# A RetNet layer with a mixture-of-depths MLP: GpSimd drained ahead of the last MLP, one-hot rows ahead of values, another order of the first choice, and a limit on loads kept for the first batch alone

## The chip, the core and the metric

The kernel runs on one core of a Trainium2 chip. The core has a matrix engine (TensorE; PE in the profile, with its weight loads as PEld), a vector engine (VectorE, DVE), a scalar engine (ScalarE, ACT), GpSimd (POOL) and a queue that only issues transfers (SyncE, SP). The metric is the device time of one execution in microseconds, lower is better; a kernel is given by the median of its runs. A profile is one more execution, with a time of its own.

## What is computed

```python
# q, k, v: (8, 8, 576, 64); scale = 1/8
scores = scale * np.matmul(q, k.transpose(0, 1, 3, 2))
gamma = 1.0 - 2.0 ** (-5.0 - np.arange(H, dtype=np.float32))
Dmat = np.where(rel >= 0, gamma[:, None, None] ** rel[None, :, :], 0.0)
ret = np.matmul(scores * Dmat, v)            # (B, H, S, D) -> x: (B, S, H*D)

scores = np.einsum('bsd,d->bs', x, w_gate)   # x: (8, 576, 512)
for b in range(B):
    top_idx = np.argpartition(-scores[b], capacity)[:capacity]   # 128 of 576
    xe = x[b, top_idx]
    h = np.maximum(xe @ w1, 0.0)             # 512 -> 1024
    ye = h @ w2                              # 1024 -> 512
    g = 1.0 / (1.0 + np.exp(-scores[b, top_idx]))
    out[b, top_idx] = x[b, top_idx] + g[:, None] * ye
```

For each of eight batches: a linear attention with decay over 576 positions and eight heads, then a choice of the 128 positions with the highest gate score, an MLP on those alone, and its result added in place. All of it is in fp32.

## The kernel before

**Tiling.** A batch is cut into nine chunks of 64 positions (NC = 9), 72 chunks in all. One *step* s handles two chunks that follow each other, so there are 36 steps (NS) and a last, empty one. A batch has an odd number of chunks, so every second batch ends in the middle of a step. `ends[b]`, the step after the one that holds the last chunk of batch b, is 5, 9, 14, 18, 23, 27, 32, 36.

**A step.** `load(s)` brings q, k, v and k turned, four transfers of 256 KB through `bring` (L90) on SP's queue into one of eight `raw` buffers; the load of step s+7 is issued at the start of step s. `scaled(s)` (L137) multiplies v by decay factors on GpSimd (`vs`). `block(s)` (L195) puts the matmuls of step s on PE: the running state (`update`, `u_ps`), the scores (`sc_ps`), and, two by two in between, the products with v and state of the step before (`crosswise`, `y_ps`). ACT copies the state (`st`, L193). `masked(s)` (L218) masks the scores on DVE into `am`. `values(s-1)` (L224) scales `y_ps` into `xs` on DVE and sums each position's gate score (two `scr`, L235); `store(s-1)` (L239) writes `xs` out from GpSimd's queue.

**The choice of a batch.** `total` and `spread` lay the scores out as one row (PE, ACT). `compare` (L288, DVE) counts for every position how many are higher, in five pieces of up to 128 positions. `one_hot` (L303, DVE) turns ranks into a one-hot matrix, `rows` (L311, PE, then ACT) makes row numbers of it, `gather` (L322, GpSimd) fetches the chosen rows from the output. For the last step of a batch the compares are cut in two (`part`), joined by `joined`.

**The MLP.** `turn(b)` (L337) transposes the gathered rows on PE. `mlp(b)` (L370) appends eight *parts* to a queue: four `up` (L344), each 16 matmuls, and four `down` (L354), each 4. `some(n)` takes n parts from its front and issues them. `share` says how many parts each step takes. The last `down` of a batch is followed by DVE's `o` (L363) and an indirect scatter from GpSimd (L364). `gates(b)` (L328) makes the gate values.

**Order.** The scheduler is manual: each engine runs its instructions in the order in which the program issues them, and waits in that order. What belongs to a choice or an MLP is put in lists by step: `before` runs at the start of a step, `early` behind the step's block, values and store, `late` behind the parts of the MLP. The limit on loads is a dependency in `bring`: a transfer waits for the fourth one before it (`flying`). For a batch b from 1 to 6, with s = ends[b]: compares in `late` of steps s+1 (three) and s+2 (two), one-hot in `late` of s+2, row numbers and gather in `before` of s+3, the turn in `early` of s+4, parts from s+5. For batch 0: first compares behind step 4, rows and gather at the start of step 7, the turn in step 8. Behind step 36 come the second half of the choice of batch 7 between the parts of batch 6's MLP, then batch 7's MLP with nothing beside it.

At the end the program has, on every engine, instructions that it adds by itself (L547): drains and semaphores by which the engines meet, and SP's waits for the last transfers.

Of the kernel before, what the change touches and what calls it, by code (L numbers as in the profile page):

```python
# [9 lines left out]
F32 = mybir.dt.float32  # L10
# [3 lines left out]
OP = mybir.AluOpType  # L14
# [21 lines left out]
def kernel(  # L36
# [39 lines left out]
    def bank(name, tag="mm", bufs=3):  # L76
        return psum.tile([P, 512], F32, tag=tag, bufs=bufs, name=name)
# [2 lines left out]
    halves = [slice(0, C), slice(C, P)]  # L80
    where = lambda e, h: slice(W * e + D * h, W * e + D * h + D)
    batch = lambda g: divmod(g, NC)

    ctx.enter_context(tc.manual_schedule(engines=ENGINES))

# [1 line left out]

    flying = deque()

    def bring(out, in_):  # L90

        ins = nc.sync.dma_start(out=out, in_=in_).ins
        if len(flying) == 4:
            tc.add_manual_dep(
                ins, flying.popleft().name,
                mybir.DependencyInfo(mybir.DependencyClass.Sync, mybir.DependencyReason.DATA),
                reason="few transfers at a time")
        flying.append(ins)

    def load(s):  # L100
        x = loads.tile([P, 4, DM], F32, name="raw")
        for a in range(4):
            bring(x[:, a, :], qkvk[s, :, a * DM : (a + 1) * DM])
        raw[s] = x

    table = const.tile([P, col["end"]], F32, name="table")
# [27 lines left out]

    vs, am, sc_ps, y_ps, u_ps, st, xs, sc = {}, {}, {}, {}, {}, {}, {}, {}

    def scaled(s):  # L137
        c = batch(2 * s)[1]
        vs[s] = work.tile([P, DM], F32, name="vs")
        nc.gpsimd.tensor_tensor(  # L140
            out=blocks(vs[s]), in0=blocks(raw[s][:, 2, :]),
            in1=dec[:, 0, HH * c : HH * c + H].unsqueeze(2).to_broadcast([P, H, D]), op=OP.mult,
        )
# [22 lines left out]
                        raw[s][half, 0, where(e, h)],  # L166
                        start=True, stop=True, skip_group_check=True)

    def crosswise(s):
        y_ps[s] = bank("y_ps", "y", 2)  # L170
        for e in range(2):
            for h in range(HH):
                for i, half in enumerate(halves):
                    yield lambda e=e, h=h, i=i, half=half: nc.tensor.matmul(  # L174
                        y_ps[s][halves[1 - i], where(e, h)], am[s][half, where(e, h)],
                        vs[s][half, where(e, h)],
                        start=e == 0 and h == 0, stop=False, skip_group_check=True)
        for e in range(2):
            g = 2 * s + e
            if batch(g)[1] == 0:  # L180
                continue
            for h in range(HH):
                for i, half in enumerate(halves):
                    yield lambda g=g, e=e, h=h, i=i, half=half: nc.tensor.matmul(  # L184
                        y_ps[s][halves[1 - i], where(e, h)], raw[s][half, 0, where(e, h)],
                        st[g - 1][half, where(0, h)], start=False, stop=True,
                        skip_group_check=True)
# [7 lines left out]
    def block(s, cross=True):  # L195

        def diagonal():
            if s:
                yield from update(2 * s - 1)
            if s < NS:  # L200
                yield from scores(s)
                yield from update(2 * s)
        a = diagonal()
        b = crosswise(s - 1) if s and cross else iter(())
        n = 0
        while True:
            some = [f for f in (next(a, None), next(a, None), next(b, None), next(b, None)) if f]
            if not some:
                break
            for f in some:  # L210
                f()
            n += 1
            if n == HH and s:
                copied(2 * s - 1)
        if s < NS:
            copied(2 * s)

    def masked(s):  # L218
        am[s] = work.tile([P, DM], F32, name="am")
        nc.vector.tensor_tensor(  # L220
            out=blocks(am[s]), in0=blocks(sc_ps[s]),
            in1=causal.unsqueeze(1).to_broadcast([P, H, C]), op=OP.mult)

    def values(s):  # L224
        c = batch(2 * s)[1]
        xs[s] = work.tile([P, DM], F32, name="xs", bufs=4)
        nc.vector.tensor_tensor(  # L227
            out=blocks(xs[s]), in0=blocks(y_ps[s]),
            in1=dec[:, 1, HH * c : HH * c + H].unsqueeze(2).to_broadcast([P, H, D]), op=OP.mult)
        for e in range(2):  # L230
            b, c = batch(2 * s + e)
            if c == 0:
                sc[b] = work.tile([P, NC], F32, name="sc", bufs=2)
            scr = work.tile([P, W], F32, name="scr", bufs=1)
            nc.vector.scalar_tensor_tensor(scr, xs[s][:, W * e : W * e + W], 1.0, wgh,  # L235
                                           op0=OP.mult, op1=OP.mult,
                                           accum_out=sc[b][:, c : c + 1])

    def store(s):  # L239
        (b, c), (b2, _) = batch(2 * s), batch(2 * s + 1)  # L240
        for i, half in enumerate(halves):
            x = xs[s][half, :].rearrange("p (c d) -> p c d", c=2)
            if b == b2:
                nc.gpsimd.dma_start(  # L244
                    out=outs[b][C * c : C * c + 2 * C, W * i : W * i + W]
                    .rearrange("(c p) d -> p c d", c=2), in_=x)
            else:
                nc.gpsimd.dma_start(out=outs[b][C * c : C * c + C, W * i : W * i + W],
                                    in_=x[:, 0, :])
                nc.gpsimd.dma_start(out=outs[b2][:C, W * i : W * i + W], in_=x[:, 1, :])  # L250
# [127 lines left out]

    before, early, late = {}, {}, {}

    def plan(when, s, f, *a):
        when.setdefault(s, []).append((f, a))
# [3 lines left out]
            f(*a)  # L388

    columns = lambda k0, k1: [(k, 0, size(k)) for k in range(k0, k1)]  # L390
    ends = [(NC * b + NC - 1) // 2 + 1 for b in range(B)]
    last = B - 1
    odd = (NC - 2) // 2


    s = ends[0]
    plan(early, s - 1, total, 0, 0, NC - 1)
    plan(early, s - 1, spread, 0, columns(0, full))
    for k in range(full):
        plan(late, s - 1, compare, 0, k, 0, P * full)  # L400
    plan(early, s, total, 0, NC - 1, NC)
    plan(early, s, spread, 0, columns(full, NK))
    for k in range(full):
        plan(late, s, compare, 0, k, P * full, S, 1)
    plan(late, s, compare, 0, full)
    plan(late, s, joined, 0, full)
    plan(late, s, one_hot, 0)
    plan(before, s + 2, rows, 0)
    plan(before, s + 2, gather, 0)
    plan(early, s + 3, turn, 0)  # L410
    plan(early, s + 3, mlp, 0)
    plan(late, s + 3, gates, 0)
    start = [s + 3]
    for b in range(1, last):
        s = ends[b]
        plan(late, s, total, b)
        plan(early, s + 1, spread, b, columns(0, full), columns(full, NK))
        for k in range(NK):
            plan(late, s + 1 + (k > 2), compare, b, k)
        plan(late, s + 2, one_hot, b)  # L420
        plan(before, s + 3, rows, b)
        plan(before, s + 3, gather, b)
        plan(early, s + 4, turn, b)
        plan(late, s + 4, mlp, b)
        plan(late, s + 4, gates, b)
        start.append(s + 5)
    plan(late, NS - 1, total, last, 0, NC - 2)
    plan(before, NS, spread, last, columns(0, odd) + [(odd, 0, C)])
    for k in range(odd):
        plan(before, NS, compare, last, k, 0, C * (NC - 2))  # L430

    share = {}
    for s0, s1 in zip(start, start[1:]):
        n = s1 - s0
        for i in range(n):
            share[s0 + i] = 8 * (i + 1) // n - 8 * i // n

    AHEAD = 8
    bring(table, consts)
# [7 lines left out]
    for s in range(NS + 1):  # L447
        if s and s + AHEAD - 1 < NS:
            load(s + AHEAD - 1)
        if s == 2:  # L450
            for d in range(0, FB, 2):
                bring(w2_sb[:, d : d + 2, :],
                      w2[P * d : P * d + 2 * P].rearrange("(a p) d -> p a d", p=P))
        run(before, s)
        if s + 1 < NS:
            scaled(s + 1)
        block(s, s != ends[0])
        if s < NS:
            masked(s)
        if s and s != ends[0]:  # L460
            values(s - 1)
            store(s - 1)
        if s == ends[0] - 1:
            for f in crosswise(s):
                f()
        if s == 2:
            nc.vector.tensor_copy(out=place, in_=place_f)
        run(early, s)
        some(share.get(s, 0))
        if s == ends[0] - 1:  # L470
            values(s)
            store(s)
        run(late, s)
    some(1)
    total(last, NC - 2, NC)
# [11 lines left out]
    some(2)  # L487
    turn(last)
    some(len(parts))
    gates(last)  # L490
    mlp(last)
    some(len(parts))
# [58 lines left out]
```

## Time and profile before

| what | us |
|---|---|
| median of three runs (286.45, 288.38, 289.0) | 288.38 |
| the profiled execution | 286.14 |
| its span, first to last instruction | 284.4 |
| PE busy in it | 233.2 |
| DVE busy | 140.8 |
| GpSimd busy | 107.2 |
| ACT busy | 53.9 |

The difference between the profiled execution and its span, 1.7 us, lies outside the program's own instructions. PE's busy time counts matmuls that overlap; it is not work at full rate. The slices and windows below give busy time by stage, the granted clock is the share of TensorE's full clock, and the DMA share is the mean busy share of the core's 16 DMA engines. In a view of waits, a row names who waited, for whom, and the total, the number and the longest of the waits. An L with a number is a line of the kernel.

The groups of instructions whose durations the text uses:

```profile
L350 PE MATMUL h_ps<-xg,w_sb 128*128 128x128 f32 x512 | 64.0, 283 | 0.8 <-ACT xg L342 0.7
L140 POOL TENSOR_TENSOR vs<-raw,table 128x512 f32<-128x512 f32 x36 | 38.8, 1078 | 41.4 <-DMA raw<-in_qkvk 34.8
L227 DVE TENSOR_TENSOR xs<-y_ps,table 128x512 f32<-128x512 f32 x36 | 24.6, 684 | 8.1 <-PE y_ps L184 7.3
L364 POOL DMA_INDIRECT out<-o,idx x8 | 9.5, 1188 | 35.0 <-DVE o L363 29.3
```

In each row: line, engine, operation, what it writes and reads, shape, count; then busy us and mean ns of one; then the engine's idle time before it and who ended it. Matmuls of one group overlap, so a part of the MLP (16 of L350, or 4 of L358) takes 1.98 us of PE in the timeline, not 16 times 283 ns.

### The profile page before, as it was taken

The numbers are of one execution on the slowest core, as the hardware profiler recorded it, in microseconds if no ns is written. First come the engines' busy times: TensorE is split into PE (matmuls) and PEld (weight loads), VectorE is DVE, ScalarE is ACT, GpSimd is POOL, SyncE is SP. The second block draws the span as 40 slices with busy tenths as digits, with TensorE's granted clock in tenths as the row PEclk, the third lists the DMA queues.
The fourth block names the chain that finished last, engine by engine and source line by source line (L and its number), as shares of the span: only waits on it lengthen the run. The fifth ranks groups of instructions, "written<-read, shape, count | busy, mean of one in ns | idle before, by whom it ended". The sixth has DMA issues, their size and how long they took to land.

```text
span 284.4 us, 11522 instructions
## 1 busy us (share of the span) xinstructions
PE 233.2 (82%) x5184; PEld 186.5 (66%) x5184; DVE 140.8 (50%) x353; ACT 53.9 (19%) x158; POOL 107.2 (38%) x141
## 2 busy tenths in 40 slices
PE   1666773798789697999999979999999889999940
PEld 1656662697566696659866966688669856866710
DVE  0455793435746376456645773576366844331010
ACT  1111211132211131122211321132113212211100
POOL 4263722603663534343446516251647231111010
PEclk9998979579999998999999998999999999999996
DMA  6788999897888988988888855771313130201000
GB/s 218 237 275 294 293 318 345 273 362 252 279 289 281 309 261 265 300 289 277 256 307 269 293 200 180 268 223 42 76 44 96 38 85 13 76 11 63 2 37 0
DMA packets 27601, 56.83 MB, mean 200 GB/s; under 512 B 4000, under 2 KB 4128, under 8 KB 27552
## 3 DMA queue, kind: packets, MB, share of 16 engines
q1 hardware_dynamic: 22688, 42.46, 46.7%
q0 software_dynamic: 4864, 13.64, 14.1%
q8 instruction: 41, 0.67, 1.0%
q14 instruction: 8, 0.07, 0.1%
HBM read 44.54 MB, written 11.53 MB: 197 GB/s over the span
## 4 chain that ended last, share of the span: by engine, by line
PE 48%; DMA 23%; issue 14%; DVE 9%; POOL 2%; POOLq 1%; ACT 0%; DVEq 0%
DMA raw<-in_qkvk 18%; PE ye_ps L358 13%; PE h_ps L350 10%; PE u_ps L154 8%; PE sc_ps L164 7%; DMA w_sb<-in_w 4%; DVE scr L294 4%; PE row_ps L281 4%; PE y_ps L184 3%; PE y_ps L174 2%; DVE scr L235 2%; DVE xs L227 2%; DVE hot L307 1%; PE xg_ps L341 1%; DMA table<-in_consts 1%
## 5 line engine op out<-in xcount | busy, mean ns | idle before, releaser
L244 POOL DMA_DIRECT2D out<-xs x64 | 39.9, 625 | 67.6 <-DVE xs L227 67.2
L350 PE MATMUL h_ps<-xg,w_sb 128*128 128x128 f32 x512 | 64.0, 283 | 0.8 <-ACT xg L342 0.7
L220 DVE TENSOR_TENSOR am<-sc_ps,table 128x512 f32<-128x512 f32 x36 | 24.9, 691 | 76.5 <-PE sc_ps L164 56.8
L350 PEld LDWEIGHTS h_ps<-xg,w_sb 128*128 128x128 f32 x512 | 60.5, 196 | 3.3 <-ACT xg L342 1.1
L358 PE MATMUL ye_ps<-w_sb,hT 128*128 128x512 f32 x128 | 59.0, 601 | 0.5 <-issue 0.5
L164 PE MATMUL sc_ps<-raw 64*64 64x64 f32 x1152 | 45.9, 232 | 13.4 <-DMA raw<-in_qkvk 11.0
L154 PE MATMUL u_ps<-vs,raw 64*64 64x64 f32 x1024 | 46.7, 232 | 9.5 <-issue 4.5
L140 POOL TENSOR_TENSOR vs<-raw,table 128x512 f32<-128x512 f32 x36 | 38.8, 1078 | 41.4 <-DMA raw<-in_qkvk 34.8
L164 PEld LDWEIGHTS sc_ps<-raw 64*64 64x64 f32 x1152 | 41.5, 147 | 15.8 <-issue 15.8
L174 PE MATMUL y_ps<-vs,am 64*64 64x64 f32 x1152 | 47.0, 234 | 5.0 <-DVE am L220 3.2
L154 PEld LDWEIGHTS u_ps<-vs,raw 64*64 64x64 f32 x1024 | 38.6, 144 | 17.1 <-issue 9.8
L294 DVE SCALAR_TENSOR_TENSOR scr<-row,rs,ahead 128x576 f32<-128x576 f32 (+5 forms) x47 | 42.1, 895 | 12.2 <-ACT row L286 10.8
L174 PEld LDWEIGHTS y_ps<-vs,am 64*64 64x64 f32 x1152 | 40.7, 145 | 5.8 <-DVE am L220 3.1
L184 PE MATMUL y_ps<-st,raw 64*64 64x64 f32 x1024 | 41.5, 230 | 0.5 <-issue 0.5
L193 ACT COPY st<-u_ps 128x256 f32<-128x256 f32 x64 | 23.8, 372 | 91.9 <-PE u_ps L154 55.8
L358 PEld LDWEIGHTS ye_ps<-w_sb,hT 128*128 128x128 f32 x128 | 23.2, 192 | 23.7 <-issue 23.2
L184 PEld LDWEIGHTS y_ps<-st,raw 64*64 64x64 f32 x1024 | 37.6, 146 | 0.9 <-issue 0.8
L235 DVE SCALAR_TENSOR_TENSOR scr<-xs,table 128x256 f32<-128x256 f32 x72 | 32.4, 450 | 2.5
L227 DVE TENSOR_TENSOR xs<-y_ps,table 128x512 f32<-128x512 f32 x36 | 24.6, 684 | 8.1 <-PE y_ps L184 7.3
L363 DVE SCALAR_TENSOR_TENSOR o<-ye_ps,gate,xr 128x512 f32<-128x512 f32 x8 | 6.0, 751 | 34.1 <-PE ye_ps L358 21.4
L364 POOL DMA_INDIRECT out<-o,idx x8 | 9.5, 1188 | 35.0 <-DVE o L363 29.3
L352 ACT ACTIVATE hT<-h_ps 128x256 f32<-128x256 f32 x32 | 12.3, 384 | 49.6 <-PE h_ps L350 49.6
(34 smaller groups left out, 105.2 us busy)
## 6 DMA issues: line engine op xcount, KB each, us to landing
raw<-in_qkvk SPq DMA_DIRECT2D x144, 256.0 KB, 4.5
out<-xs POOLq DMA_DIRECT2D x64, 128.0 KB, 4.9
w_sb<-in_w SPq DMA_DIRECT2D x8, 512.0 KB, 5.5
out<-xs POOLq DMA_DIRECT2D x16, 64.0 KB, 5.1
wg<-in_w_gate SPq DMA_DIRECT2D x1, 256.0 KB
table<-in_consts SPq DMA_DIRECT2D x1, 234.5 KB
xr<-out,idx POOLq DMA_INDIRECT x8, 5.5
out<-o,idx POOLq DMA_INDIRECT x8
```

What stands on the lines that cost most here:

```text
L140: nc.gpsimd.tensor_tensor(out=blocks(vs[s]), in0=blocks(raw[s][:, 2, :]), in1=dec[:, 0, HH * c : HH * c + H].unsqueeze(2).to_broadcast([P, ...
L154: yield lambda h=h, half=half: nc.tensor.matmul(u_ps[b][half, where(0, h)], raw[s][half, 3, where(e, h)], vs[s][half, where(e, h)], start= ...
L164: yield lambda e=e, h=h, half=half: nc.tensor.matmul(sc_ps[s][half, where(e, h)], raw[s][half, 1, where(e, h)], raw[s][half, 0, where(e, h ...
L174: yield lambda e=e, h=h, i=i, half=half: nc.tensor.matmul(y_ps[s][halves[1 - i], where(e, h)], am[s][half, where(e, h)], vs[s][half, where ...
L184: yield lambda g=g, e=e, h=h, i=i, half=half: nc.tensor.matmul(y_ps[s][halves[1 - i], where(e, h)], raw[s][half, 0, where(e, h)], st[g - 1 ...
L220: nc.vector.tensor_tensor(out=blocks(am[s]), in0=blocks(sc_ps[s]), in1=causal.unsqueeze(1).to_broadcast([P, H, C]), op=OP.mult)
L227: nc.vector.tensor_tensor(out=blocks(xs[s]), in0=blocks(y_ps[s]), in1=dec[:, 1, HH * c : HH * c + H].unsqueeze(2).to_broadcast([P, H, D]), ...
L235: nc.vector.scalar_tensor_tensor(scr, xs[s][:, W * e : W * e + W], 1.0, wgh, op0=OP.mult, op1=OP.mult, accum_out=sc[b][:, c : c + 1])
L244: nc.gpsimd.dma_start(out=outs[b][C * c : C * c + 2 * C, W * i : W * i + W] .rearrange("(c p) d -> p c d", c=2), in_=x)
L294: nc.vector.scalar_tensor_tensor(scr[:n, : j1 - j0], row[b][:n, j0:j1], rs[b][:n, k : k + 1], ahead[:n, at + j0 : at + j1], op0=OP.subtrac ...
L350: nc.tensor.matmul(t[:, a, :], w1_sb[:, d, P * (f + a) : P * (f + a) + P], xg[b][:, d, :], start=d == 0, stop=d == KD - 1)
L358: nc.tensor.matmul(ye[b], hT[b][:, a, :], w2_sb[:, a, :], start=a == 0, stop=a == FB - 1)
```

## The change

Seven things, of which none changes what is computed:

1. `bring` gets an argument `few`. Only the loads of steps up to `ends[0]` = 5 wait for the fourth transfer before them; later loads and all weights don't.
2. `vs` of steps 5, 6 and 7 is made by ACT, in eight pieces a step, in place of GpSimd.
3. `crosswise` and `values` can do one chunk of a step alone, and steps 4 and 5 are written out as `first` and `second`: the chunk that ends batch 0 comes ahead of the one that begins batch 1, whose values stand behind batch 0's one-hot.
4. Batch 0's row numbers and gather go to step 6, its turn to step 7; its parts are taken from step 8 on, as before.
5. For batches 1 to 6 the last two compares and the one-hot go from behind a step's parts to ahead of its values (a new list, `mid`); row numbers and gather go from the start of the next step to the end of this one, behind the parts.
6. `mlp(b)` is queued in the step of its turn, and the shares are dealt earlier in each stretch, at most two a step, with the last part of a batch in the step in which the next batch's begin.
7. GpSimd drains between the scatter of batch 6 and the MLP of batch 7.

```diff
-    def bring(out, in_):
+    def bring(out, in_, few=False):
         ins = nc.sync.dma_start(out=out, in_=in_).ins
-        if len(flying) == 4:
+        while len(flying) > 3 + few:
+            flying.popleft()
+        if few and len(flying) == 4:
             tc.add_manual_dep(
...
-            bring(x[:, a, :], qkvk[s, :, a * DM : (a + 1) * DM])
+            bring(x[:, a, :], qkvk[s, :, a * DM : (a + 1) * DM], few=s <= ends[0])
...
+    by_act = lambda s: ends[0] <= s < ends[0] + 3
+
     def scaled(s):
...
+        if by_act(s):
+            for i in range(H):
+                nc.scalar.activation(
+                    out=vs[s][:, D * i : D * i + D], in_=raw[s][:, 2, D * i : D * i + D],
+                    func=AF.Copy, scale=dec[:, 0, HH * c + i : HH * c + i + 1])
+            return
...
-    def crosswise(s):
-        y_ps[s] = bank("y_ps", "y", 2)
-        for e in range(2):
+    def crosswise(s, es=(0, 1)):
+        if es[0] == 0:
+            y_ps[s] = bank("y_ps", "y", 2)
+        for e in es:
...
-    def values(s):
+    def values(s, es=(0, 1)):
...
+    def first():
+        s = ends[0] - 1
+        block(s)
+        masked(s)
+        go(crosswise(s, (0,)))
+        values(s - 1)
+        store(s - 1)
+        total(0, 0, NC - 1)
+        spread(0, columns(0, full))
+        values(s, (0,))
+        total(0, NC - 1, NC)
+        spread(0, columns(full, NK))
+        go(crosswise(s, (1,)))
+        for k in range(full):
+            compare(0, k, 0, P * full)
+
+    def second():
+        s = ends[0]
+        block(s, False)
+        masked(s)
+        for k in range(full):
+            compare(0, k, P * full, S, 1)
+        compare(0, full)
+        joined(0, full)
+        one_hot(0)
+        values(s - 1, (1,))
+        store(s - 1)
...
-    plan(before, s + 2, rows, 0)
-    plan(before, s + 2, gather, 0)
-    plan(early, s + 3, turn, 0)
-    plan(early, s + 3, mlp, 0)
-    plan(late, s + 3, gates, 0)
-    start = [s + 3]
+    s = ends[0] + 1
+    plan(mid, s, rows, 0)
+    plan(mid, s, gather, 0)
+    plan(early, s + 1, turn, 0)
+    plan(late, s + 1, mlp, 0)
+    plan(late, s + 1, gates, 0)
+    start = [s + 2]
     for b in range(1, last):
         s = ends[b]
...
-        for k in range(NK):
-            plan(late, s + 1 + (k > 2), compare, b, k)
-        plan(late, s + 2, one_hot, b)
-        plan(before, s + 3, rows, b)
-        plan(before, s + 3, gather, b)
+        for k in range(3):
+            plan(late, s + 1, compare, b, k)
+        for k in range(3, NK):
+            plan(mid, s + 2, compare, b, k)
+        plan(mid, s + 2, one_hot, b)
+        plan(late, s + 2, rows, b)
+        plan(late, s + 2, gather, b)
         plan(early, s + 4, turn, b)
-        plan(late, s + 4, mlp, b)
+        plan(early, s + 4, mlp, b)
         plan(late, s + 4, gates, b)
-        start.append(s + 5)
+        start.append(s + 4)
...
     share = {}
-    for s0, s1 in zip(start, start[1:]):
-        n = s1 - s0
-        for i in range(n):
-            share[s0 + i] = 8 * (i + 1) // n - 8 * i // n
+    for i, (s0, s1) in enumerate(zip(start, start[1:])):
+        n = 0
+        for s in range(s0, s1 + 1):
+            most = 1 if s == s1 or (i and s == s0) else 2
+            more = min(most, 8 - n - (s1 - s))
+            share[s] = share.get(s, 0) + more
+            n += more
...
-        if s + 1 < NS:
+        if s + 1 < NS and not by_act(s + 1):
             scaled(s + 1)
...
+        if s == ends[0] - 1:
+            first()
+        elif s == ends[0]:
+            second()
+        else:
+            block(s)
+            if s < NS:
+                masked(s)
+            run(mid, s)
+            if s:
+                values(s - 1)
+                store(s - 1)
...
+        if by_act(s + 1):
+            scaled(s + 1)
         run(early, s)
         some(share.get(s, 0))
         run(late, s)
...
     some(len(parts))
+    nc.gpsimd.drain()
     gates(last)
     mlp(last)
     some(len(parts))
```

More of the change, by code (lines that the diff above doesn't have):

```diff
@@ L82 @@
     batch = lambda g: divmod(g, NC)
+    ends = [(NC * b + NC - 1) // 2 + 1 for b in range(B)]
     ctx.enter_context(tc.manual_schedule(engines=ENGINES))
@@ L177, in crosswise @@
                         start=e == 0 and h == 0, stop=False, skip_group_check=True)
-        for e in range(2):
+        for e in es:
             g = 2 * s + e
@@ L222, in masked @@
             in1=causal.unsqueeze(1).to_broadcast([P, H, C]), op=OP.mult)
-    def values(s):
+    def values(s, es=(0, 1)):
         c = batch(2 * s)[1]
-        xs[s] = work.tile([P, DM], F32, name="xs", bufs=4)
+        if es[0] == 0:
+            xs[s] = work.tile([P, DM], F32, name="xs", bufs=4)
+        i0, i1 = HH * es[0], HH * es[-1] + HH
         nc.vector.tensor_tensor(
-            out=blocks(xs[s]), in0=blocks(y_ps[s]),
-            in1=dec[:, 1, HH * c : HH * c + H].unsqueeze(2).to_broadcast([P, H, D]), op=OP.mult)
-        for e in range(2):
+            out=blocks(xs[s])[:, i0:i1, :], in0=blocks(y_ps[s])[:, i0:i1, :],
+            in1=dec[:, 1, HH * c + i0 : HH * c + i1].unsqueeze(2).to_broadcast([P, i1 - i0, D]),
+            op=OP.mult)
+        for e in es:
             b, c = batch(2 * s + e)
@@ L377, in some @@
             f(*a)
-    before, early, late = {}, {}, {}
+    before, mid, early, late = {}, {}, {}, {}
     def plan(when, s, f, *a):
@@ L390, with go @@
     columns = lambda k0, k1: [(k, 0, size(k)) for k in range(k0, k1)]
-    ends = [(NC * b + NC - 1) // 2 + 1 for b in range(B)]
     last = B - 1
     odd = (NC - 2) // 2
[L396 to L407, printed above, removed]
-    plan(before, s + 2, rows, 0)
-    plan(before, s + 2, gather, 0)
-    plan(early, s + 3, turn, 0)
-    plan(early, s + 3, mlp, 0)
-    plan(late, s + 3, gates, 0)
-    start = [s + 3]
+    def go(fs):
+        for f in fs:
+            f()
+    def first():
[31 more added lines that the diff above has]
+    start = [s + 2]
     for b in range(1, last):
@@ L432 @@
     share = {}
-    for s0, s1 in zip(start, start[1:]):
-        n = s1 - s0
-        for i in range(n):
-            share[s0 + i] = 8 * (i + 1) // n - 8 * i // n
+    for i, (s0, s1) in enumerate(zip(start, start[1:])):
[5 more added lines that the diff above has]
+            n += more
+        assert n == 8
     AHEAD = 8
@@ L454 @@
         run(before, s)
-        if s + 1 < NS:
+        if s + 1 < NS and not by_act(s + 1):
             scaled(s + 1)
[L457 to L462, printed above, removed]
-        if s == ends[0] - 1:
-            for f in crosswise(s):
-                f()
+        if s == ends[0] - 1:
+            first()
[9 more added lines that the diff above has]
+                store(s - 1)
         if s == 2:
             nc.vector.tensor_copy(out=place, in_=place_f)
+        if by_act(s + 1):
+            scaled(s + 1)
         run(early, s)
         some(share.get(s, 0))
-        if s == ends[0] - 1:
-            values(s)
-            store(s)
         run(late, s)
```

## The prediction

> **What bounds the kernel now.** First the page's slices (7.1 us each): which engine is full in which stage.
>
> ```profile
> PE   1666773798789697999999979999999889999940
> PEclk9998979579999998999999998999999999999996
> DMA  6788999897888988988888855771313130201000
> ```
>
> From about the tenth slice on PE is full; before it, while the first loads come, it has holes. The last slice is empty: something behind the last matmul. So three stages, each read alone. The chain of waits for 40 to 67 us (start, length, what):
>
> ```profile
> 39.33 6.17 DMA w_sb<-in_w
> 45.52 4.82 DMA raw<-in_qkvk
> 50.36 4.10 DMA raw<-in_qkvk
> 54.47 5.77 DMA w_sb<-in_w
> 60.26 5.33 DMA raw<-in_qkvk
> 65.76 1.05 POOL vs L140
> ```
>
> Up to 65.8 us nothing but loads is on the path: step 8's load, step 9's, w2, step 10's. What the engines did there (busy times of PE, PEld, DVE, ACT, POOL; then the granted clock, the DMA share, GB/s):
>
> ```profile
> 40.00:50.00 10.00, 4.80 (x237) 4.10 (x234) 5.08 (x14) 1.65 (x5) 2.29 (x3) 1.00 0.96 348
> 50.00:65.00 15.00, 12.29 (x246) 11.04 (x235) 5.11 (x14) 4.16 (x10) 4.79 (x6) 0.66 0.91 311
> 65.00:111.00 46.00, 38.13 (x964) 31.26 (x965) 28.48 (x69) 9.21 (x27) 21.64 (x28) 1.00 0.86 280
> ```
>
> PE is half idle to 50, then works 12.3 of 15 us at a clock of 0.66. From 65 it is the bound: a load comes every 4.8 us, a step takes about 6.6 (block 10 starts at 65.1, block 35 at 229.5). What still stops it there, first from the waits of PE, then in the chain:
>
> ```profile
> PE idx_ps L315 <- DVE hot L307: 9.1, 7, 2.1
> ```
> ```profile
> 74.34 0.06 DVE am L220
> 74.95 0.69 DVE xs L227
> 75.67 0.44 DVE scr L235 x2
> 76.13 0.43 DVE scr L235 x2
> 76.56 0.75 DVE scr L294 x2
> 77.34 0.82 DVE scr L294 x2
> 78.16 0.61 DVE hot L307
> 78.82 0.37 PE idx_ps L315 x5
> ```
>
> PE's part of the MLP ends at 76.69 and PE waits 2.13 us for the one-hot, ahead of which DVE does the values of the step (xs and two scr: 1.6 us). The timeline has four such stops of 2.06 to 2.13 us (78.8, 110.9, 169.8, 228.7 us), 8.3 of the 9.1. Last, the instructions of the program's end (duration min/median/max, first and last start):
>
> ```profile
> L547 POOLq DRAIN  x3: 40/108/9130, 274.4 to 284.1; - x3
> L547 SPq DRAIN  x3: 7/7/7, 278.0 to 283.8; - x3
> ```
>
> GpSimd's first drain takes 9.13 us from 274.43, to 283.56. SP, which waits for the last scatter to land, is through at 278.0. So 5.5 us of the end are GpSimd's drain alone.
>
> **The change part by part.**
>
> *Drain ahead of the last MLP.* It adds a drain between the scatter of batch 6 (issued 260.60, 1.18 us) and that of batch 7 (274.66), which waits for DVE's o. Behind it on POOL is only that last scatter. Cover: 274.66 - 261.78 = 12.9 us. Scatters and gathers don't keep GpSimd: in the timeline a vs (L140) that follows an indirect one, and has its load, starts 1.02 to 1.26 us after it. So the 9.13 us are 1.2 us of scatter, the landing, and some 6 us of something else. The two drains behind it, with no transfer in between, took 108 and 40 ns. What one costs after a single transfer the trace does not show. If the time is per transfer since the start (96), the early drain takes it in the cover and the last one only waits for the landing: the end follows SP, -5.5. If it is owed behind any transfer, 0. A loss would need an early drain over 12.9 us; the one seen is 9.1. I take -5.5: its nearest rows are the short drains, which show that a drain as such is cheap.
>
> *Few loads for batch one only.* Before, each transfer on SP waits for the fourth before it. After, from step 6's loads on, that wait is gone; as built, SP's transfers take turns on eight semaphores, so each waits for the eighth before it: 2 MB in flight instead of 1 (SP's next wait, for a free raw buffer, is not near: it fills seven steps ahead). The four 512 KB pieces of w1 already had 2 MB in flight, in the window with share 0.96. The other windows are 0.89 (28 to 40 us) and 0.91 (50 to 65). Filled to 0.96: 12 x 0.07 + 15 x 0.05 = 1.6 us earlier for step 10's load (bounds 0, and 3.1 if filled to 1.00). It lands near 63.4 instead of 65.1.
>
> *First choice, and vs of steps 5 to 7 on ACT.* Half of the cross products and values of step 4 move behind the choice (DVE: half of 0.69, one scr of 0.44 with its 0.08: about 0.9 us), and the row numbers come in step 6, not 7. The gather, issued at 43.9, comes 3 to 4 us earlier and lands about 45; the turn (0.66 us of PE) moves from step 8 to the end of step 7. The 24 ACT pieces of 128x64, at the 217 ns of ACT's copy of that shape, take 1.74 us a step against 1.08 on POOL; if vs came last, that is 0.66 us each, so 0 to 2 us, or a small gain where DVE's compares no longer meet POOL's vs (one took 2.18 us at 32.5, its neighbours 0.75). I take 0: block 6 waits for DVE, blocks 7 and 8 for loads. By itself the choice is worth nothing for the end, loads being last.
>
> *Parts of the MLP.* Shares of batch 0 go from 1,1,2,1,1,2 (steps 8 to 13) to 2,2,1,1,1,1: two more parts of 1.98 us ahead of block 10. Is there room? From block 8 (49.3, some 0.9 earlier with the loads): two blocks of 2.1, four parts, 0.8 us of sums and gaps, 12.9 in all: block 10 could start at 61.3 and waits for its load until 63.4. With the half clock as before (10 us at half, 5 us of work lost) it starts at 66.3. Gain: 3.96 + 1.7 = 5.7, or 3.96 - 1.2 = 2.8. I take 4.5. From there PE is the bound and keeps it.
>
> *One-hot ahead of values.* In each choice of batches 1 to 6, compares and one-hot stand 1.6 us earlier on DVE; as built, the row numbers keep their place on PE, between a part and the next block, and the gather its place on POOL, ahead of the next vs. The four stops of 2.07 go to about 0.45: 6.4 us. The values behind come 2.5 us later; stores on POOL wait for them, and the gather behind the stores, so the gather gets little earlier. PE needs the freed y_ps two blocks later: no stop.
>
> *The clock.* The half clock of 3.4 us starts at 111.7 and at 169.7, right behind two of these stops (they end at 110.9 and 169.8); each loses 1.7 us of work. The Trainium skill, "TensorE: Matmul & The Clock Gate", Part 1, says the clock falls after an idle window of about 3.4 us; by that a 2 us stop should not do it and removing it would save nothing. The row shows the fall with 2 us of idle, so up to 3.4 us could come back; two other stops had none. I take 1.5.
>
> *The gathers.* Turn waits for the gather: in batch 1 it is issued at 79.66 and turned at 86.02, 6.4 us later, and it lands in
>
> ```profile
> DMA to landing us min/median/max: 4.7/5.5/6.1
> ```
>
> so slack is about 1 us, in other batches up to 3. If the spread of 1.4 us is what four loads in flight cost, eight make 7.5 at the most: a stop of about 1 us in some batches. The Trainium skill speaks against such a loss: "DMA: Bandwidth & Descriptors", Queues, rings and completion order, has each DMA engine take turns between its queues packet by packet, so a longer load queue would cost a gather nothing. By the rule 0, by the row up to -5 over four batches while loads run; I take a loss of 2.
>
> *Sum*: 5.5 + 4.5 + 6.4 + 1.5 - 2 = 15.9 us. The profiled execution took 286.14 (span 284.4); it becomes 270.2. The median shown is 288.38, 2.2 above it, so 272.5.
>
> **The rivals.** (1) The drain's time is owed behind the last transfer whatever was drained before. For: only one long drain is seen. Against: the short ones. 288.4 - 10.4 = 278. (2) The stops move: the one-hot is early, but late values, masks and gathers stop PE in its place, as DVE has 4.9 us in a one-part step of 4.5. Then 4.5 + 5.5 remain: 278.5. (3) Slower: gathers queue behind eight loads. Place: turn on PE, with a block behind it. 2 MB at 290 GB/s are 7 us, landing 12.5; less about 1.5 us of slack and the 5.5 known, 5.5 us each for batches 1 to 4, and 3 us in batch 0 (turn now stands ahead of block 8): 25 us against 17.9 of gains, 295.5. It decides from a landing of about 10.6 us. Against: landings never passed 6.1, with four loads in flight. (4) Neither drain nor stops give anything and the front alone is left, 4.5 - 2: 286, no change.
>
> **How the numbers follow.** Forecast 0.47, (1) 0.24, (2) 0.12, (3) 0.10, (4) 0.07. 1% (2.9 us) is about what a measurement of this kernel can tell. Faster 0.83, within 0.07, slower 0.10. The range, 263 to 284, takes in the drain at 0, the front at 2.8, and below the forecast the full 3.4 us of clock, no gather loss and a filled DMA; outside are (3), (4) and 0.05 below.
>
> **What would show it.** Right: the last drain under 3 us and the early one about 9, inside the last MLP; two parts more ahead of block 10; idx stops under 0.6 us. Wrong: a last drain of 6 us or more; gathers over 7 us with PE waiting at L341's like; block 10 not earlier in work done.

## The result, and the profile after

The changed kernel takes 274.1 us (median of four runs, 272.9 to 275.1), the kernel before 288.7 (four runs, 286.5 to 292.4). The ratio is 0.952, with a 95% interval of 0.944 to 0.960: faster, by 14.6 us between the medians where 15.9 were forecast. The profiled execution of the changed kernel took 274.87 us (span 273.2), so between the two profiled executions there are 11.3 us. Medians take in all runs and ratios only those within 1.5% of their kernel's fastest; two experiments below (the one-hot alone, and both edits with limited loads) have a slower run as their profile, so of the first only waits are read and of the second only the count of stops at the end.

The slices of the changed kernel (6.8 us each):

```profile
PE   1845886089977999969999999699999998999992
PEclk9998568569998999999999999979999999999998
DMA  6879999999996786586577766866042113211000
```

The front is not fuller than before: the eighth slice of PE is empty, and the fourth to the ninth have a granted clock under 0.9. The DMA engines are full from the fourth to the twelfth. The windows that were shown of before:

```profile
40.00:50.00 10.00, 5.37 (x213) 4.50 (x205) 6.54 (x20) 4.15 (x17) 2.82 (x5) 0.76 1.03 383
50.00:65.00 15.00, 9.37 (x256) 8.78 (x260) 3.12 (x9) 3.47 (x7) 6.57 (x9) 0.70 1.05 393
65.00:111.00 46.00, 42.61 (x1040) 33.79 (x1030) 27.91 (x66) 10.15 (x31) 19.23 (x25) 0.96 0.81 272
```

(A share over 1 means that counted times of packets overlap.) From 50 to 65 us loads run at 393 GB/s in place of 311, and PE is busy for less, 9.4 us in place of 12.3. From 65 on it is busier, 42.6 of 46 us in place of 38.1. The waits of PE say where the front went:

```profile
PE xg_ps L356 <- DMA xr<-out,idx: 12.6, 4, 7.5
PE sc_ps L175 <- DMA raw<-in_qkvk: 5.9, 1, 5.9
PE idx_ps L330 <- DVE hot L322: 3.2, 4, 1.4
```

Loads hold up PE once, at the very first block. Stops ahead of the row numbers are down from 9.1 us to 3.2. New is the first row: PE waits 12.6 us for gathered rows, 7.5 of it at once. The chain of waits has it as a transfer, ahead of the turn of batch 0:

```profile
48.73 6.85 DMA xr<-out,idx
55.63 1.11 PE xg_ps L356 x4
```

And the end, the early drain first, then those of the program's end:

```profile
L534 POOLq DRAIN  x1: 9263/9263/9263, 254.7 to 254.7; - x1
...
L592 POOLq DRAIN  x3: 46/108/3035, 268.8 to 272.9; - x3
L592 SPq DRAIN  x3: 7/7/7, 272.3 to 272.6; - x3
```

The early drain takes 9.3 us between the two scatters, the last one 3.0 and ends at 271.8, ahead of SP (272.3). DVE's last `o` starts at 268.0, 5.2 us before the end of the span; in the kernel before it started at 273.6, 10.7 us before the end.

### The profile page after: what moved, and what is told of

It is laid out like the page before. It is cut to its first block, busy times and chain, and to the rows that moved or that the text cites. A ratio compares the mean times of both kernels' runs of the same rounds, so it can differ in the third digit from the quotient of the medians.

```text
span 273.2 us, 11548 instructions
## 1 busy us (share of the span) xinstructions
PE 231.0 (85%) x5184; PEld 183.9 (67%) x5184; DVE 141.7 (52%) x354; ACT 58.7 (22%) x182; POOL 103.3 (38%) x138
## 4 chain that ended last, share of the span: by engine, by line
PE 60%; issue 14%; DMA 13%; DVE 8%; ACT 1%; POOLq 1%; POOL 1%; SPq 0%; DVEq 0%; ACTq 0%
PE h_ps L365 17%; PE ye_ps L373 11%; PE u_ps L165 9%; PE sc_ps L175 9%; DMA xr<-out,idx 7%; DVE scr L309 5%; DMA raw<-in_qkvk 5%; PE row_ps L296 5%; PE y_ps L196 4%; PE y_ps L186 3%; PE xg_ps L356 2%; DVE hot L322 1%; DVE am L232 1%; DMA out<-xs 1%; PE idx_ps L330 1%
## 5 line engine op out<-in xcount | busy, mean ns | idle before, releaser
L365 PEld LDWEIGHTS h_ps<-xg,w_sb 128*128 128x128 f32 x512 | 59.5, 192 | 5.5 <-issue 4.4
L373 PE MATMUL ye_ps<-w_sb,hT 128*128 128x512 f32 x128 | 63.0, 624 | 0.0
L365 PE MATMUL h_ps<-xg,w_sb 128*128 128x128 f32 x512 | 62.2, 278 | 0.5 <-issue 0.4
L175 PE MATMUL sc_ps<-raw 64*64 64x64 f32 x1152 | 44.9, 231 | 11.0 <-DMA raw<-in_qkvk 5.9
L186 PE MATMUL y_ps<-vs,am 64*64 64x64 f32 x1152 | 45.9, 232 | 3.0 <-issue 2.7
L165 PEld LDWEIGHTS u_ps<-vs,raw 64*64 64x64 f32 x1024 | 38.1, 144 | 11.7 <-issue 6.4
L196 PE MATMUL y_ps<-st,raw 64*64 64x64 f32 x1024 | 39.7, 227 | 2.0 <-issue 2.0
L151 POOL TENSOR_TENSOR vs<-raw,table 128x512 f32<-128x512 f32 x33 | 34.7, 1052 | 13.3 <-DMA raw<-in_qkvk 12.8
L196 PEld LDWEIGHTS y_ps<-st,raw 64*64 64x64 f32 x1024 | 36.0, 143 | 2.1 <-issue 2.1
L250 DVE SCALAR_TENSOR_TENSOR scr<-xs,table 128x256 f32<-128x256 f32 x72 | 34.0, 473 | 2.5
L241 DVE TENSOR_TENSOR xs<-y_ps,table 128x512 f32<-128x512 f32 (+1 forms) x37 | 24.7, 667 | 3.9 <-PE y_ps L196 3.6
L367 ACT ACTIVATE hT<-h_ps 128x256 f32<-128x256 f32 x32 | 12.3, 383 | 55.7 <-PE h_ps L365 55.7
```

The costliest lines, as they stand in the source:

```text
L151: nc.gpsimd.tensor_tensor(out=blocks(vs[s]), in0=blocks(raw[s][:, 2, :]), in1=dec[:, 0, HH * c : HH * c + H].unsqueeze(2).to_broadcast([P, ...
L165: yield lambda h=h, half=half: nc.tensor.matmul(u_ps[b][half, where(0, h)], raw[s][half, 3, where(e, h)], vs[s][half, where(e, h)], start= ...
L175: yield lambda e=e, h=h, half=half: nc.tensor.matmul(sc_ps[s][half, where(e, h)], raw[s][half, 1, where(e, h)], raw[s][half, 0, where(e, h ...
L186: yield lambda e=e, h=h, i=i, half=half: nc.tensor.matmul(y_ps[s][halves[1 - i], where(e, h)], am[s][half, where(e, h)], vs[s][half, where ...
L241: nc.vector.tensor_tensor(out=blocks(xs[s])[:, i0:i1, :], in0=blocks(y_ps[s])[:, i0:i1, :], in1=dec[:, 1, HH * c + i0 : HH * c + i1].unsqu ...
L365: nc.tensor.matmul(t[:, a, :], w1_sb[:, d, P * (f + a) : P * (f + a) + P], xg[b][:, d, :], start=d == 0, stop=d == KD - 1)
```

## The experiments

Each time stands beside runs of the kernel before on the same chip. On the three chips these had medians of 288.5, 290.4 and 291.0 us, so from chip to chip ratios are the better measure. "Block 10 starts" means its first scores, the first matmul that needs step 10's load.

**One part of the change at a time, on the kernel before.**

*The drain alone* (the diff is the one line `nc.gpsimd.drain()` ahead of `gates(last)`).

> The kernel before with the early drain alone. Theory (a drain pays for each transfer since the last one, the early one lies in the cover of the last MLP): last drain about 3 us, the early one about 9, time 5.5 us below before: 283 against 288.5. Rival (the 11 us of the whole change have little to do with it): under 3 us.

285.96 us, ratio 0.989 (0.982 to 0.996). The end of its profile:

```profile
L548 POOLq DRAIN  x3: 46/108/3043, 275.5 to 279.6; - x3
L548 SPq DRAIN  x3: 7/7/7, 279.1 to 279.4; - x3
```

The last drain is 3.0 us, as forecast, and GpSimd is ready ahead of SP. From the start of the last `o` to the end of the span there are 5.2 us, 5.5 less than before: the end gives what was forecast. The two profiled spans differ by 4.5 us, the medians by 4.4, the ratio says 1.2 to 5.1: 5.5 lies just outside. In this profile the loads of the front were later (step 10's landed at 68.0 us), which takes some of it back.

*The loads alone.*

```diff
-        if len(flying) == 4:
+        while len(flying) > 3 + few:
+            flying.popleft()
+        if few and len(flying) == 4:
...
-            bring(x[:, a, :], qkvk[s, :, a * DM : (a + 1) * DM])
+            bring(x[:, a, :], qkvk[s, :, a * DM : (a + 1) * DM], few=s <= 5)
```

> The kernel before with the limit on loads kept for steps 0 to 5 alone. Theory (loads bind the front of the kernel before, and with eight in flight they run at 360 to 390 GB/s there): step 10's load lands near 58 us in place of 64.7, block 10 starts about 5 us earlier, time 4 to 6 us below before. Rival (the wait moves to the turn of batch 0, whose gather now shares the engines with more loads, as in the changed kernel): block 10 starts at 64 or later, time within 2 us of before.

289.69 us, ratio 0.998 (0.989 to 1.007): nothing. The loads did speed up,

```profile
50.00:65.00 15.00, 13.65 (x328) 12.63 (x327) 5.54 (x15) 4.16 (x10) 5.60 (x7) 0.69 1.04 389
```

and step 10's landed at 57.3 us in place of 64.7; but block 10 started at 63.4, only 1.7 earlier, since PE was still at the parts and block 9 (granted clock 0.69). Up to 65 us PE also stood 9.1 us in stops that nothing in the profile explains, where before it stood 4.2 (the last section counts them). By 113 us, in batch 2's choice, the profile is 2.2 us behind that of before, after a stop of 4.2 us at 99.9 (told of at the end) and two more stretches of half clock. So where theory put the gain, PE itself was next, not a transfer; the rival named the turn of batch 0, and there PE did not wait.

*One-hot ahead of the values alone.*

```diff
-        for k in range(NK):
-            plan(late, s + 1 + (k > 2), compare, b, k)
-        plan(late, s + 2, one_hot, b)
-        plan(before, s + 3, rows, b)
-        plan(before, s + 3, gather, b)
+        for k in range(3):
+            plan(late, s + 1, compare, b, k)
+        for k in range(3, NK):
+            plan(mid, s + 2, compare, b, k)
+        plan(mid, s + 2, one_hot, b)
+        plan(late, s + 2, rows, b)
+        plan(late, s + 2, gather, b)
```

> The kernel before with, for batches 1 to 6, the last two compares and the one-hot ahead of the values and row numbers and gather behind the parts, nothing else. Theory: the four stops of 2.07 us of PE before the row numbers fall to 0.6 (6 us less), but the gathers go out 1.5 to 2 us later and PE stops at some turns: 3 to 5 us in all, so 1 to 3 us net, 286. Rival (no gather stop here): 6 us or more, 282.

286.31 us, ratio 0.985 (0.979 to 0.991), 4 us. Its waits of PE:

```profile
PE xg_ps L341 <- DMA xr<-out,idx: 5.3, 4, 2.9
...
PE idx_ps L315 <- DVE hot L307: 2.2, 4, 0.6
```

6.9 us of stops went ahead of the row numbers, and 4.9 came back at the turns (0.4 before). The first is as the theory has it, the second at the top of its 3 to 5. The net of 1 to 3 us was too low: the ratio says 2.5 to 6.2, so 2 lies outside.

*The shares of the parts alone.*

```diff
-        plan(late, s + 4, mlp, b)
+        plan(early, s + 4, mlp, b)
...
-        start.append(s + 5)
+        start.append(s + 4)
...
-        for i in range(n):
-            share[s0 + i] = 8 * (i + 1) // n - 8 * i // n
+        n = 0
+        for s in range(s0, s1 + 1):
+            most = 1 if s == s1 or (i and s == s0) else 2
+            more = min(most, 8 - n - (s1 - s))
+            share[s] = share.get(s, 0) + more
+            n += more
```

> The kernel before with the earlier shares of the MLP's parts alone (and a batch's parts queued in the step of its turn). Theory (two more parts ahead of block 10 fit into the time in which loads bind): four parts done when block 10 starts, block 10 not over 1 us later than at 65.1, 3 to 4 us below before. Rival (PE has no room there, as in the changed kernel): block 10 starts 3 to 4 us later and the time is within 1 us of before.

282.19 us, ratio 0.976 (0.967 to 0.985): the largest single part, 4 to 10 us. Block 10 starts at 65.8 us with four parts done, where before it started at 65.1 with two, and the window tells why there was room:

```profile
50.00:65.00 15.00, 14.33 (x243) 13.58 (x236) 5.10 (x14) 3.85 (x8) 3.95 (x6) 0.74 0.92 301
```

PE is busy 14.3 us of 15, before 12.3: the two parts fill the wait for step 10's load. They are 3.96 us, less the 0.7 by which block 10 is later: 3.2 of the 6.7 us between the two profiled spans. The other 3.5 come behind block 10, where the shares moved too; no run divides them.

**One part of the change taken back.** *All transfers limited to four, in the changed kernel* (`few` True for every transfer).

> The changed kernel with the limit of four kept for all transfers. Theory (in the changed kernel the front is bound by the turn of batch 0, not by loads): step 10's load lands near 65 us, ahead of block 10 (69.6 us in the changed kernel), time within 2 us of 274.1. Rival (the loads carry the gain of the front): block 10 later and 4 us or more above it, 278 to 280.

274.86 us, ratio 0.948 (0.936 to 0.959): the same as the changed kernel. Step 10's load landed at 66.1, ahead of block 10 at 68.6. PE's wait for gathered rows is 5.9 us longer and the time no worse; the unexplained stops of the last section are 3.8 us in this profile in place of 10.1.

```profile
PE xg_ps L356 <- DMA xr<-out,idx: 18.5, 6, 9.5
```

**What holds up the gathers.** GpSimd in the changed kernel's timeline, for batch 0:

```profile
30.98 0.53 POOL L263 DMA_DIRECT2D out<-xs  x1 [0.42 <-DVE xs L241]
42.19 0.53 POOL L265 DMA_DIRECT2D out<-xs  x1 [10.68 <-DVE xs L241]
42.71 0.52 POOL L263 DMA_DIRECT2D out<-xs  x1
43.22 0.52 POOL L265 DMA_DIRECT2D out<-xs  x1
48.73 1.03 POOL L339 DMA_INDIRECT xr<-out,idx  x1 [4.99 <-ACT st L205]
```

The store of step 4 is four transfers: half of batch 0's last chunk (L263), half of batch 1's first (L265), and the two other halves. The second waits 10.7 us for the values that now stand behind the one-hot, and the third, which batch 0's gather needs, stands behind it. The row numbers are there at 42.5; the gather waits for that store to land, at 47.8, and goes at 48.73. (The view names ACT's `st`, which ended by chance just before: in the four profiles with this order the gather goes 0.94 or 0.95 us after the landing of the third transfer, and 0.2 to 1.5 us after an `st`.) The fix:

```diff
         values(s, (0,))
+        store(s, (0,))
...
         values(s - 1, (1,))
-        store(s - 1)
+        store(s - 1, (1,))
```

> The changed kernel, with the store of step 4 cut in two: the chunk that ends batch 0 is stored (two transfers) right behind its own values, the chunk that begins batch 1 behind its values. Theory (the gather of batch 0 waits for a store that stands behind the late values): the gather, issued at 48.7 us in the changed kernel, goes out by 44, lands by 49, PE's wait at the turn of batch 0 falls from 7.5 to under 1.5 us, and the time is 4 to 8 us below the changed kernel's 274.1: about 268. Rival (the wait at the turn only covers a wait for loads or for the clock): PE's wait moves to block 8 or 9, and the time stays at 272 to 275.

The gather goes at 39.86,

```profile
28.89 1.05 POOL L260 DMA_DIRECT2D out<-xs  x2
38.39 1.03 POOL L260 DMA_DIRECT2D out<-xs  x2 [8.45 <-DVE xs L241]
39.86 1.27 POOL L345 DMA_INDIRECT xr<-out,idx  x1 [0.44 <-issue]
```

PE's wait at the turn of batch 0 is 1.3 us, not 7.5, and block 10 starts at 62.2 in place of 70.2. From row numbers to gather there are 0.7 us in place of 6.3, so the cause of the wait is settled. But the row numbers too were 3.2 us earlier in this profile (39.2 us, behind 3.4 us of half clock in place of 13.7), so not all of the gain at block 10 is the store's. The time is 272.9 us, ratio 0.950 (0.943 to 0.957): 1.2 us less than the changed kernel by medians, inside the spread. By the two profiles the span is 4.3 less; of 8.0 us ahead at block 10, half was given back by batch 2's turn (116.9 against 121.1 us).

*Gathers ahead of the step's store*, in the six steps where a choice ends:

```diff
+    held = {ends[b] + 2 for b in range(1, last)}
...
                 values(s - 1)
-                store(s - 1)
+                if s not in held:
+                    store(s - 1)
...
         run(late, s)
+        if s in held:
+            store(s - 1)
```

> The changed kernel, with the store of the step held back behind the row numbers and the gather in the six steps in which a choice of batches 1 to 6 ends. Theory (the late values hold up the store on GpSimd's queue, and the store the gather): gathers go out 1.5 to 2 us earlier, the waits of PE at the turns of batches 2 and 4 (2.2 and 2.6 us) fall under 0.5, the half clock behind the second goes: 4 to 6 us less than 274.1, about 269. Rival (the gathers are late because of loads in flight, landing time decides): the waits stay over 1.5 us and the time is 273 to 275.

270.78 us, ratio 0.940 (0.932 to 0.949). PE's waits at the turns:

```profile
PE xg_ps L356 <- DMA xr<-out,idx: 7.7, 2, 7.3
```

All but batch 0's 7.3 are gone, and so is the half clock behind the fourth batch's. The profile shows the order that did it, in batch 2 with the changed kernel first, then this one:

```profile
113.61 1.23 POOL L259 DMA_DIRECT2D out<-xs  x2 [7.26 <-DVE xs L241]
115.14 1.02 POOL L339 DMA_INDIRECT xr<-out,idx  x1 [0.30 <-PE y_ps L196]
```
```profile
113.76 1.27 POOL L339 DMA_INDIRECT xr<-out,idx  x1 [7.07 <-ACT idx L333]
115.04 1.23 POOL L259 DMA_DIRECT2D out<-xs  x2
```

*Both.*

> Both edits together, batch 0's store ahead and the six gathers ahead of the step's store. Theory: the gains add, 262 to 267. Rival: one hides the other or loads bind next: no better than the better of the two alone.

265.86 us, ratio 0.924 (0.916 to 0.931): 8 us less than the changed kernel, the fastest version here with its limit on loads as changed. By medians the store gives 1.2 alone, the gathers 3.3, both 8.2, more than the sum; by the profiled spans 4.3, 4.5 and 9.7. That fits what the store's gain met alone, the late turn of batch 2, which the gathers' edit takes away. PE waits 1.6 us for gathered rows in all:

```profile
PE xg_ps L362 <- DMA xr<-out,idx: 1.6, 2, 1.3
```

*Both, with all transfers limited.*

> The kernel with batch 0's store ahead and the six gathers ahead of the step's store (265.9), with the limit of four kept for all transfers. Theory (in the changed kernel the faster loads were hidden behind the turn of batch 0; with that stop gone they count): step 10's load lands near 65 us and block 10 starts there in place of 61.2, so 3 to 5 us more: 269 to 271. Rival (faster loads are worth nothing anywhere): 265 to 267.

266.52 us, ratio 0.910 (0.899 to 0.922). By medians the same as without the limit, by ratios if anything faster. The two were run on different chips, and the intervals overlap: whether the faster loads are worth anything once the turn does not bind stays open. No run here shows a gain from them.

**What a drain pays for.**

```diff
         run(late, s)
+        if s == 17:
+            nc.gpsimd.drain()
```

> The changed kernel with one more drain on GpSimd at the end of step 17, behind 42 of the 96 transfers; 53 follow up to the second drain, one up to the last. Theory (a drain takes some 65 ns for each transfer since the drain before it): the new drain about 2.7 us plus the landing of what is in flight, the second falls from 9.3 to 6.2 to 7 us, the last stays at 3.0. Rival (the first drain pays some 6 us once, whatever its count): the new one 6 us or more plus landing, the second about 3. The time may rise, as the vs of a step waits behind the new drain.

The two early drains:

```profile
L519 POOLq DRAIN  x1: 9043/9043/9043, 117.5 to 117.5; - x1
```
```profile
L536 POOLq DRAIN  x1: 5824/5824/5824, 254.6 to 254.6; - x1
```

The first looks like the rival's, but most of it is waiting: instructions ahead of it ran until 119.4, and the last packet of their transfers was written at 124.3; it ended at 126.5. The second fell from 9.3 to 5.8, somewhat more than expected. Counted from the last packet to the drain's end:

| kernel | transfers since the drain before | us from last packet to end |
|---|---|---|
| this one, last drain | 1 | 0.4 |
| this one, first | 42 | 2.2 |
| this one, second | 53 | 3.0 |
| changed, early | 95 | 6.4 |
| before, last | 96 | 6.5 |

It grows with the count, by some 45 to 65 ns a transfer. GpSimd's other instructions do not order it (25 ahead of the 2.2 us, 17 ahead of the 3.0); the time since the drain before grows along with the count in these rows, so transfers and time are not told apart. The rival (6 us once) would have had 6 and 0.4 in the second and third row. The time, one run of 274.8 us, did not rise.

## Why the prediction held, point by point

- **Drain, -5.5**: right. From `o` to the end there are 5.2 us in place of 10.7. The prediction chose the case in which a drain pays for what came since the drain before, and the table shows that it does. Alone it measured 1.2 to 5.1.
- **Loads, 1.6 us earlier for step 10's**: the term was sized at 1.6, with 3.1 as its bound, and measured 6.7 (64.7 to 58.0). The step that failed is that a share of 0.96 or 1.00 was taken as the ceiling at an unchanged rate: at a share of 1.04 the engines moved 389 GB/s, where 0.91 had been 311, so bytes rose more than the share. It made no difference to the time: alone nothing, taken back nothing. What the prediction did not have is that PE stops more with eight loads in flight (last section).
- **First choice, "lands about 45", worth 0**: this step failed. The gather went at 48.7, later than the 43.9 of before, and landed at 55.6. The prediction went through GpSimd's queue for the gather and not for the store of step 4, whose four transfers alternate between the two batches. PE stood 7.5 us with block 8 behind it; the half clock of 13.7 us from 45.2 covers it. ACT took 2.0 us a step for `vs`, where 1.74 were reckoned. Neither `vs` on ACT nor the new order of the first choice was run alone, so that the first is worth 0 is not shown.
- **Parts, +4.5 at block 10**: the room was there (four parts by 65.8 us in the experiment), but in the whole change block 10 starts at 70.2, 5.1 us later than before with 3.96 us of parts more done: about -1.1 in place of 4.5. The stop at the turn took it.
- **One-hot, 6.4**: right; 9.1 to 3.2 is 5.9 us. Three of the four stops left are 0.6 us, as foretold; batch 1's is 1.4.
- **The clock, 1.5**: measured 0. From 65 us on there are again two stretches of half clock of 3.4 us, at 86.2 and 178.3, next to stops of 2.0 and 2.6 us. The prediction held its row against the rule of the Trainium skill ("TensorE: Matmul & The Clock Gate", Part 1), by which it takes an idle window of about 3.4 us. Half clock behind shorter stops is seen again, and again not behind every one: 2.2 us at 121.1 had none.
- **The gathers, -2**: the size was too small and the cause another. The turns of batches 1 to 7 cost 5.1 us, 4.8 of it in batches 2 and 4. Landings did not get slower with eight loads in flight. The row of before, 4.7 to 6.1 us, rests on three of the eight gathers, those of batches 1, 3 and 5, which took 5.5, 6.1 and 4.7 us; in the changed kernel the same three took 3.5, 5.1 and 4.0. Batch 0's took 6.9, and over all profiles landings reach 7.7 us with four loads in flight and with eight. It was the late store ahead of the gather, which the prediction had written down ("the gather gets little earlier") and not priced. The rule that queues take turns (the Trainium skill, "DMA: Bandwidth & Descriptors", Queues, rings and completion order) agrees with the landings; it does not speak of this wait.

The terms were reckoned on profiles, and by the two profiled spans 15.9 us met 11.2: the end gave 5.5, the stretch from block 10 to `o` 10.7, and block 10 came 5.1 later. Of the 10.7, 3.96 are the two parts done before, 1.1 the one-hot's 5.9 less the turns' 4.8. The other 5.7 are no term of the prediction; with the shares alone the same stretch was shorter by 3.5 beyond the two parts, and what is left no run divides. So three terms were wrong: the front by 5.6 us, the gathers by 3 and the clock by 1.5, all too favourable, and a gain that was not reckoned stood against them. That the medians lie 14.6 apart, within 1.3 of the forecast, is luck in part: the profiled execution of before was 2.5 us under its kernel's median, that of the changed kernel 0.8 over.

The slower rival, gathers behind loads, is refuted by the landings: it decides from 10.6 us, and none passed 7.7. The rival of moved stops was half true: the stops moved to the turns and took 4.8 of the one-hot's 5.9 us, until the gathers went ahead of the store.

## What to carry over

When work is moved on one engine, follow what its results feed on every queue: here values were put behind the one-hot, a store waited for them, and a gather that was to come earlier stood behind the store. A store that serves two consumers is cut so that the urgent half goes out first. If GpSimd issues many transfers, look for its drain at the end, and drain once where it has nothing to do. And when loads get faster, look at what else waits: here the DMA engines were fuller, and no time was gained.

## What was not expected of the hardware

- GpSimd's drain takes longer the more transfers GpSimd has issued since the drain before it: behind the landing of the last one 0.4 us after one transfer, 6.5 after 96, some 45 to 65 ns for each (table above; the time since then may be what counts).
- From 4 to 8 transfers of 256 KB in flight took the loads from 311 to 393 GB/s (50 to 65 us), with a DMA share of 0.91 and 1.05.
- PE stops with all it needs at hand by the profile, its wait put down to `issue`: 2.4 us in the kernel before, 2.0 in the changed one (and 4.2 with the loads alone).

```profile
99.29 0.27 PE L154 MATMUL u_ps<-vs,raw 64*64 64x64 f32 x1 [2.37 <-issue]
```
```profile
84.93 0.33 PE L196 MATMUL y_ps<-st,raw 64*64 64x64 f32 x3 [1.99 <-issue]
```

These are PE's 1999th matmul in the old order and its 1618th in the new one. The twelve profiles have 54 such stops of over 0.6 us, and every one stands at the 222nd, 349th, 476th matmul and so on, in steps of 127, give or take one. The queue that carries instructions moved 41 packets of 16 KB in each profile:

```profile
q8 instruction: 41, 0.67, 1.0%
```

PE's 5184 matmuls in steps of 127 make 41 too. So PE stops where one block of its program ends, and most likely waits for the next; that is argued, not shown, as no run changed how the program comes in. The stops (of 0.4 us and more) are longer with more loads in flight: 8.7 to 15.0 us in the six profiles with eight, 11.1 on average, and 2.7 to 9.9, 5.5 on average, in the six with four. That may be why the faster loads gave nothing: with the loads alone the stops were 15.0 us in place of 7.4.
